# Moving one batch's attention under the weight loads, and spacing attention steps evenly, in a fused attention and feed-forward kernel

## The chip, the cores and the metric

The kernel runs on one core of one Trainium2 chip. The metric is the time of one execution on the device in microseconds (us). Every time below is the median of several executions. A profile is one execution, and its span is about 2 us shorter than the time that the same execution is given as a run. All instants below are us from the start of that span.

Engines are named as in the profile: PE is the matrix engine, DVE the vector engine, ACT the scalar engine, POOL is GpSimd, and SPq is the queue that issues most of the loads.

## The reference

Sliding-window causal attention with a window of 64, then LayerNorm and a two-layer feed-forward with a residual:

```python
# q, k, v: (8, 8, 576, 64) float32;  g_ln: (512,);  w_ch1: (512, 2048);  w_ch2: (2048, 512)
rel    = pos[:, None] - pos[None, :]
mask   = (rel >= 0) & (rel < 64)
scores = np.where(mask, q @ k.T / 8, -1e9)           # per batch and head
x      = softmax(scores) @ v                         # -> (8, 576, 512), heads side by side
xn     = (x - mean(x)) / sqrt(var(x) + 1e-6) * g_ln
out    = x + np.maximum(xn @ w_ch1, 0) @ w_ch2       # (8, 576, 512) float32
```

## The kernel before

The 8 x 576 rows are 36 blocks of 128 rows (`kblk`), in nine groups of four. A batch is 4.5 blocks, so a batch ends in the middle of a block. All matrix products are in float16.

A group's feed-forward is 32 units of four matmuls of 512 columns each: 16 units of layer 1 (`hps`, one per 128 hidden channels) and 16 of layer 2 (`ch`, four per block). The attention of the next batch is put between the units. `at(i, f)` means: issue `f` after unit `i`. In these traces an engine's instructions begin in the order in which they are issued: in the kernel before, for example, a cast on GpSimd whose data had landed at 59.23 us began at 60.84 us, after the cast issued before it (58.76 to 60.65); and PE began layer 2 at 62.38 us, after transposes issued before it, though the last cast of W2 had ended at 54.39 us and the last Relu at 56.48.

```python
    def s_mm(b, ws):            # scores of up to two windows of 64, all heads, then exp on ACT
        ...
    def s_mask(b, ws):          # DVE: pt = pt * mask
        ...
    def b_step(kblk):           # PE: xps = pt @ [v, 1]; then on DVE, one after the other:
        ...                     #   rcp, xn = xps * rcp, bn_stats, bn_aggr, z = (xn - mean) * g
    def zt_step(kblk, eng=None):# PE: transposes z; DVE (or ACT) copies the result to zT
        ...
    for g in range(NGRP):
        units = mlp_units(g)
        ...
        b = g + 1
        at(13, group_stats, g)                      # 1/sqrt(var) of the group, mostly on GpSimd
        if g == 0:
            at(12, t_rem, 0)                        # transposes of batch 0's last 64 rows of q, k
            at(12, cast_qk_rem, 1)
            ...
            t0, s0, sp = 10, 20, 2                  # batch 1 in group 0: steps of 2 units, from 20 on
        else:
            t0, s0, sp = 0, 6, 3                    # steps of 3 units, at 6, 9, 12, 15, 18
        if b < B:
            ...
            for i, ws in enumerate(sets):           # five sets: [0], [1,2], [3,4], [5,6], [7,8]
                at(s0 + sp * i, s_mm, b, ws)
                at(s0 + sp * i + 1, s_mask, b, ws)
            for kblk in range(first, last):
                si = s0 + sp * ((lastw + 1) // 2) + 3
                at(min(si, 32), b_step, kblk)
                at(max(min(si + 4, 32), 17 if kblk // 4 > b else 0), zt_step, kblk)
        if b + 1 < B:                               # loads and GpSimd casts of the batch after that
            ...
            at(22, load_v, n, 0, 4)
            ...
            at(30, cast_v, n, 0, 4)
```

Before group 0, GpSimd is given, in this order: the casts of W1, of batch 1's q and k, of batch 0's remainder, of W2, and of batch 1's V. In the prologue the shifted copy of V (`vB`: the same rows, moved by 64 partitions) is made by DMA from the cast `vA`.

The softmax here doesn't subtract the row's maximum and nothing guards it: scores larger than these inputs give would overflow.

## Time and profile before

The time before is 387.1 us (three runs, 386.42 to 387.87). The timeline of PE gives the first matmul of layer 1 of each group:

| group | 0 | 1 | 2 | 3 | 4 | 5 | 6 | 7 | 8 | end of PE |
|---|---|---|---|---|---|---|---|---|---|---|
| start, us | 37.02 | 92.04 | 132.30 | 171.30 | 209.64 | 248.65 | 286.99 | 324.48 | 352.25 | 380.18 |
| length, us | 55.02 | 40.26 | 39.00 | 38.34 | 39.01 | 38.34 | 37.49 | 27.77 | 27.93 | |

Group 7 has no attention to do. Its 128 matmuls of 512 columns take 27.77 us, or 217 ns each. PE is busy for all of the 27.77 us, at a granted clock of 1.00, and no group is shorter. That is taken here as PE's floor.

The page of the kernel before. First the busy time of each engine and its share of the span. Then the clock that PE was granted, in tenths of full speed, in 40 equal slices. Last, by engine, the chain of waits that ended last:

```profile
PE 323.3 (84%) x2768; PEld 162.6 (42%) x2768; DVE 189.6 (49%) x350; ACT 140.4 (37%) x247; POOL 121.9 (32%) x216
...
PEclk9999996996999999999999999999999999999999
...
PE 55%; DVE 26%; DMA 8%; SPq 6%; issue 3%; POOL 1%; ACT 0%; POOLq 0%
```

DVE is busy for only half of the span, yet it holds a quarter of the chain of waits. So it is the limit in stretches, not on average. The two sixes in the clock are the slices around 60 and 90 us: PE stood still there, and then ran at a lower clock.

The wait view of the kernel before, PE's waits: what waited, its line, what released it, then us in total, times, and the longest. The 5.8 us for the first load are left out:

```profile
PE tpr_697 L192 <- POOL qkr_0_1_616 L104: 5.7, 1, 5.7
PE xps_337 L238 <- DMA vB_188<-vA_133: 3.6, 1, 3.6
...
PE xps_466 L238 <- DVE pt_7_420 L221: 2.3, 1, 2.3
...
PE xps_2037 L238 <- DVE pt_7_1967 L221: 1.4, 1, 1.4
```

They belong to three stages. The second and the third are in the prologue: the V shift by DMA, and a mask. The last is one of the waits for masks (`pt`) that come back in every group from 1 to 6. The first is explained by the timeline of group 0 (start, length, engine, line, operation; in brackets the engine's idle time before it and what ended that):

```profile
58.76 1.89 POOL L125 CAST vA_276<-v_1_261 128x2048 f16<-128x2048 f32 x1 [4.14 <-DMA v_1_261<-in_v_dram]
...
60.84 0.60 POOL L104 CAST qkr_0_1_616<-qk32r_1_270 64x512 f16<-64x512 f32 x1
...
61.50 0.39 PE L192 MATMUL tpr_697<-ident_99,qkr_0_1_616 64*128 64x64 f16 x4 [5.66 <-POOL qkr_0_1_616 L104]
...
62.38 0.61 PE L315 MATMUL ch_0_708<-w2s,hrT_503 128*128 128x512 f16 x1
```

A small cast of batch 1's remainder stood on GpSimd behind the cast of a V that landed late. PE's transposes of that remainder stood in front of layer 2. So layer 2 could not start before 62.38 us.

Windows of the kernel before. The columns are length, busy time (and count) of PE, PEld, DVE, ACT and POOL, PE's granted clock, DMA share, and GB/s:

```profile
61.50:66.00 4.50, 4.33 (x19) 1.86 (x20) 0.49 (x2) 0.00 (x0) 3.75 (x13) 0.59 1.14 323
72.00:92.04 20.04, 12.21 (x179) 6.56 (x180) 19.23 (x36) 3.26 (x6) 6.44 (x10) 0.93 0.59 150
132.30:171.30 39.00, 35.37 (x341) 18.12 (x340) 24.89 (x46) 15.74 (x28) 12.34 (x23) 1.00 0.57 134
```

From 72 to 92 us DVE is busy for 19.23 of 20.04 us with batch 1's attention while PE works for 12. In group 2 PE is idle for 3.6 us of 39, spread over the waits for masks.

Three lines of the timeline of group 2 show part of why DVE is late there. In quiet places of the same trace `z` takes 0.75 us and the mask 0.69 us (for example at 75.25 and 75.92 us). Here both are longer, and GpSimd is casting beside them:

```profile
154.47 1.07 DVE L255 SCALAR_TENSOR_TENSOR z_1939<-xn_1915,mvg_1510,gB 128x512 f16<-128x512 f32 x1
...
154.94 1.50 POOL L95 CAST qk_1_4_0_2094<-qk_1_4_0_1849 128x1024 f16<-128x1024 f32 x1
...
155.46 1.52 DVE L221 TENSOR_TENSOR pt_5_1896<-pt_5_1896,mask 128x1024 f16<-128x1024 f16 x1
```

Of the group's four waits for masks, the two long ones (1.3 and 1.4 us) follow DVE instructions lengthened like this; before the other two (0.4 and 0.6 us) `z` and the mask have their usual lengths.

### The profile page before, as it was taken

The numbers are of one execution on the slowest core, as the hardware profiler recorded it, in microseconds if no ns is written. First come the engines' busy times: TensorE is split into PE (matmuls) and PEld (weight loads), VectorE is DVE, ScalarE is ACT, GpSimd is POOL, SyncE is SP. The second block draws the span as 40 slices with busy tenths as digits, with TensorE's granted clock in tenths as the row PEclk, the third lists the DMA queues.
The fourth block names the chain that finished last, engine by engine and source line by source line (L and its number), as shares of the span: only waits on it lengthen the run. The fifth ranks groups of instructions, "written<-read, shape, count | busy, mean of one in ns | idle before, by whom it ended". The sixth has DMA issues, their size and how long they took to land.

```text
span 384.1 us, 6774 instructions
## 1 busy us (share of the span) xinstructions
PE 323.3 (84%) x2768; PEld 162.6 (42%) x2768; DVE 189.6 (49%) x350; ACT 140.4 (37%) x247; POOL 121.9 (32%) x216
## 2 busy tenths in 40 slices
PE   2444985965997999799979997999799989999995
PEld 1332442433543454345434543454345444444442
DVE  1266030895369438943594379535953794002011
ACT  2421560311671177107710771077107710621610
POOL 4756748640026401630164017311722110101000
PEclk9999996996999999999999999999999999999999
DMA  8999899956301892189318920894073001002002
GB/s 253 274 322 272 304 250 270 202 133 210 71 2 46 170 280 49 34 174 259 80 32 175 294 43 23 183 237 103 24 184 90 2 29 64 19 27 84 0 27 82
DMA packets 73918, 51.62 MB, mean 134 GB/s; under 512 B 47632, under 2 KB 64016, under 8 KB 73888
## 3 DMA queue, kind: packets, MB, share of 16 engines
q1 hardware_dynamic: 72528, 46.41, 46.3%
q0 software_dynamic: 1360, 4.79, 5.8%
q8 instruction: 21, 0.34, 0.4%
q14 instruction: 9, 0.07, 0.1%
HBM read 36.96 MB, written 9.44 MB: 121 GB/s over the span
## 4 chain that ended last, share of the span: by engine, by line
PE 55%; DVE 26%; DMA 8%; SPq 6%; issue 3%; POOL 1%; ACT 0%; POOLq 0%
SPq L114 3%; DMA w1s_125<-in_moe_w_ch_dram 3%; DMA w2s_234<-in_moe_w_ch_dram 2%; DMA qk_0_1_1_214<-in_q_dram 2%; DMA qk32r_1_272<-in_k_dram 1%; PE ch_0_708 L315 1%; SPq L79 1%; PE ch_3_4604 L315 1%; PE ch_2_2087 L315 1%; PE ch_1_4564 L315 1%; PE ch_3_4413 L315 1%; PE ch_1_4373 L315 1%; PE ch_2_4196 L315 1%; PE ch_2_3667 L315 1%; PE ch_3_3185 L315 1%
## 5 line engine op out<-in xcount | busy, mean ns | idle before, releaser
L302 PEld LDWEIGHTS <-w1g 128*128 128x128 f16 x576 | 53.8, 99 | 59.4 <-issue 6.0
L315 PEld LDWEIGHTS <-hrT_4433 128*128 128x128 f16 x64 | 6.3, 98 | 7.6
L315 PEld LDWEIGHTS <-hrT_4242 128*128 128x128 f16 x64 | 6.2, 98 | 7.6
L321 DVE SCALAR_TENSOR_TENSOR osb_4370<-ch_0_4353,rstdg_4327,xn_3495 128x512 f32<-128x512 f32 x1 | 0.8, 751 | 16.2 <-PE ch_0_4353 L315 16.2
L321 DVE SCALAR_TENSOR_TENSOR osb_4561<-ch_0_4544,rstdg_4518,xn_3949 128x512 f32<-128x512 f32 x1 | 0.8, 750 | 16.2 <-PE ch_0_4544 L315 16.2
L315 PEld LDWEIGHTS <-hrT_503 128*128 128x128 f16 x64 | 5.8, 103 | 6.8 <-issue 1.9
L176 DVE COPY qkT_1_571<-tp_1_0_589 128x1024 f16<-128x1024 f16 x1 | 1.2, 1225 | 14.9 <-PE tp_1_0_589 L183 14.9
L290 POOL TENSOR_TENSOR rstmp_1316<-rstdg_1315 128x4 f32<-128x4 f32 x2 | 0.8, 386 | 24.5 <-DVE rstdg_1315 L285 24.4
L290 POOL TENSOR_TENSOR rstmp_4519<-rstdg_4518 128x4 f32<-128x4 f32 x2 | 0.4, 198 | 25.4 <-DVE rstdg_4518 L285 25.3
L315 PEld LDWEIGHTS <-hrT_3729 128*128 128x128 f16 x64 | 5.8, 98 | 6.0
L315 PEld LDWEIGHTS <-hrT_2665 128*128 128x128 f16 x64 | 5.8, 98 | 6.0
L315 PEld LDWEIGHTS <-hrT_1085 128*128 128x128 f16 x64 | 5.8, 98 | 6.0
L315 PEld LDWEIGHTS <-hrT_3213 128*128 128x128 f16 x64 | 5.8, 98 | 6.0
L315 PEld LDWEIGHTS <-hrT_1601 128*128 128x128 f16 x64 | 5.8, 98 | 6.0
L315 PEld LDWEIGHTS <-hrT_2149 128*128 128x128 f16 x64 | 5.8, 97 | 6.0
L306 ACT ACTIVATE hrT_3729<-hps_0_3730 128x512 f16<-128x512 f32 x1 | 0.6, 597 | 15.5 <-PE hps_0_3730 L302 15.5
L306 ACT ACTIVATE hrT_3213<-hps_0_3214 128x512 f16<-128x512 f32 x1 | 0.6, 597 | 15.5 <-PE hps_0_3214 L302 15.5
L306 ACT ACTIVATE hrT_2665<-hps_0_2666 128x512 f16<-128x512 f32 x1 | 0.6, 597 | 15.5 <-PE hps_0_2666 L302 15.5
L306 ACT ACTIVATE hrT_1601<-hps_0_1602 128x512 f16<-128x512 f32 x1 | 0.6, 597 | 15.5 <-PE hps_0_1602 L302 15.5
L306 ACT ACTIVATE hrT_2149<-hps_0_2150 128x512 f16<-128x512 f32 x1 | 0.6, 597 | 15.5 <-PE hps_0_2150 L302 15.5
L290 POOL TENSOR_TENSOR rstmp_2922<-rstdg_2921 128x4 f32<-128x4 f32 x2 | 0.8, 386 | 17.2 <-DVE rstdg_2921 L285 17.2
L290 POOL TENSOR_TENSOR rstmp_1858<-rstdg_1857 128x4 f32<-128x4 f32 x2 | 0.8, 386 | 17.2 <-DVE rstdg_1857 L285 17.1
(1309 smaller groups left out, 931.4 us busy)
## 6 DMA issues: line engine op xcount, KB each, us to landing
v_0_113<-in_v_dram SPq DMA_DIRECT2D x4, 256.0 KB, 7.4
v_1_261<-in_v_dram SPq DMA_DIRECT2D x4, 256.0 KB, 6.9
v_2_784<-in_v_dram SPq DMA_DIRECT2D x4, 256.0 KB, 6.3
v_3_1524<-in_v_dram SPq DMA_DIRECT2D x4, 256.0 KB, 4.4
v_4_2073<-in_v_dram SPq DMA_DIRECT2D x4, 256.0 KB, 4.5
v_5_2589<-in_v_dram SPq DMA_DIRECT2D x4, 256.0 KB, 4.3
v_6_3137<-in_v_dram SPq DMA_DIRECT2D x4, 256.0 KB, 4.3
v_7_3653<-in_v_dram SPq DMA_DIRECT2D x4, 256.0 KB, 5.8
```

Source lines behind the costliest of these rows:

```text
L79: nc.sync.dma_start(out=t[:, :].rearrange("p h j d -> p h (j d)"), in_=src[b, 4 * half:4 * half + 4, 0:512, :].rearrange("h (p j) d -> p h ...
L114: nc.sync.dma_start(out=v32[b][:, c], in_=v[b, :, 128 * c:128 * c + 128, :].rearrange("h s d -> s h d"),)
L176: nc.vector.tensor_copy(out=out, in_=in_)
L290: nc.gpsimd.tensor_tensor(out=ab, in0=rs, in1=rs, op=ALU.mult)
L302: nc.tensor.matmul(out=hps, lhsT=w1g[:, kc, 128 * hc:128 * (hc + 1)], rhs=zT[g][:, kc, :], start=(kc == 0), stop=(kc == NKC - 1),)
L306: nc.scalar.activation(out=hrT[:, hc, :], in_=hps, func=AF.Relu, bias=0.0, scale=1.0)
L315: nc.tensor.matmul(out=ch[kb], lhsT=hrT[:, hc, 128 * kb:128 * (kb + 1)], rhs=w2s[:, hc, :], start=(hc == 0), stop=(hc == NHC - 1),)
L321: nc.vector.scalar_tensor_tensor(out=o, in0=ch[kb], scalar=rstd[g][:, kb:kb + 1], in1=x_norm[kblk][:, :, :].rearrange("p h d -> p (h d)"), ...
```

## The change

The intent has four parts:

1. **Prologue.** The mask becomes a product on PE, a large negative bias written into the scores by an identity matmul, so DVE no longer multiplies masks there. DVE copies replace the DMA that shifts V.
2. **Group 0.** Batch 1's scores run during layer 1 of group 0 and its DVE chain during layer 2. Batch 1 is loaded and cast before W2. Layer 2 of group 0 runs chunk by chunk over the hidden channels in four PSUM banks, so that each chunk of W2 is used as it lands.
3. **Groups 1 to 6.** The attention steps stand five units apart (2, 7, 12, 17, 22) instead of three. Loads and casts of the next batch come earlier, and so do its transposes: they now stand in layer 2 of the group before.
4. **Evacuations.** Copies of transposes out of PSUM move from DVE to ACT.

```diff
+    def make_vB0(c):                       # the V shift, now on DVE
+        nc.vector.tensor_copy(out=vB[0][64:128, c, :, 0:D], in_=v32[0][0:64, c])
+        nc.vector.tensor_copy(out=vB[0][0:64, c + 1, :, 0:D], in_=v32[0][64:128, c])
 ...
+        if pe_mask:                        # in s_mm: the mask as a product
+            for par in range(2):
+                nc.tensor.matmul(out=sc[par]..., lhsT=ident16, rhs=mb, start=True, stop=False, ...)
 ...
+        def l2_hc(i):                      # layer 2 of group 0, two hidden chunks for all four blocks
+            if i == 0:
+                for kb in range(4):
+                    pool, tag = (ps_mm, "mm") if kb < 2 else (ps_s, "sc")
+                    ch[kb] = pool.tile([128, DM], FP32, tag=tag, name=f"ch_{g}_{kb}")
+            for hc in (2 * i, 2 * i + 1):
+                for kb in range(4):
+                    nc.tensor.matmul(out=ch[kb], lhsT=hrT[:, hc, ...], rhs=w2s[:, hc, :], ...)
+            if i == NHC // 2 - 1:
+                for kb in range(4):
+                    add_out(kb)
 ...
+    (prologue: W1, batch 1, its remainder and its V come before)
+    for i in range(8):
+        w2_load(i)
+        w2_cast(i)
 ...
         if g == 0:
+            at(8, t_main, 1, 0, 0, 1)
 ...
             at(12, t_rem, 0)
             at(12, cast_qk_rem, 1)
-            ...
-            t0, s0, sp = 10, 20, 2
+            for i, j in enumerate((12, 13, 14, 15)):
+                at(j, s_mm, 1, SETS[i])
+                at(j, s_mask, 1, SETS[i])
+                ...
+            at(20, t_rem, 1)
+            sb = [17, 18, 19, 20, 21]
+            at(17, group_stats, 0)
         else:
-            t0, s0, sp = 0, 6, 3
+            ss = [2, 7, 12, 17, 22]
+            sb = [x + 3 for x in ss]
+            at(13, group_stats, g)
 ...
-            at(22, load_v, n, 0, 4)
-            at(24, cast_qk, n, 0)
-            at(30, cast_v, n, 0, 4)
+            e = 16 if g > 0 else 12
+            at(e - 6, load_v, n, 0, 4)
+            at(e - 1, cast_qk, n, 0)
+            at(e + 5, cast_v, n, 0, 4)
+            at(e + 8, t_main, n, 0, 0, 0)   # the last argument: evacuate on ACT
 ...
```

More of the change, by code (lines that the diff above doesn't have):

```diff
@@ L64 @@
     mask = p_const.tile([128, 64], FP16, tag="mask", name="mask")
+    mbias = p_const.tile([128, 64], FP16, tag="mbias", name="mbias")
     magt = p_const.tile([128, 4], FP32, tag="magt", name="magt")
@@ L176, in evac, with t_main @@
             nc.vector.tensor_copy(out=out, in_=in_)
-    def t_main(b, x, half):
+    def t_main(b, x, half, eng=None):
         src = qk16.pop((b, x, half))
@@ L183, in t_main, with t_rem @@
                 nc.tensor.transpose(out=tp[:, i, j, :], in_=src[:, i, j], identity=ident16)
-        evac(x, qkT[b][x][:, 2 * half:2 * half + 2, 64 * x:64 * x + 512].rearrange("c i (p j) -> c i p j", j=4),
+        evac(x if eng is None else eng, qkT[b][x][:, 2 * half:2 * half + 2, 64 * x:64 * x + 512].rearrange("c i (p j) -> c i p j", j=4),
              tp[:, :].rearrange("c i j p -> c i p j"))
-    def t_rem(b):
+    def t_rem(b, eng=1):
         tp = ps_t.tile([128, 2, NHP, 64], FP16, tag="tp", name=f"tpr_{b}")
@@ L194, in t_rem, with s_mm @@
         for x in range(2):
-            nc.vector.tensor_copy(out=qkT[b][x][:, :, 64 * x + 512:64 * x + S], in_=tp[:, x])
-    def s_mm(b, ws):
+            evac(eng, qkT[b][x][:, :, 64 * x + 512:64 * x + S], tp[:, x])
+    def s_mm(b, ws, pe_mask=False):
         nw = len(ws)
@@ L200, in s_mm @@
         pt = p_pt.tile([128, 2, NHP, nw, 64], FP16, tag=f"pt{nw}", name=f"pt_{b}_{ws[0]}", bufs=6 if nw == 2 else 3)
+        if pe_mask:
+            m = mbias[:, :]
+            mb = bass.AP(tensor=m.tensor, offset=m.offset, ap=[m.ap[0], [0, NHP * nw], m.ap[1]])
+            for par in range(2):
+                nc.tensor.matmul(
+                    out=sc[par][:, :].rearrange("p h w i -> p (h w) i"), lhsT=ident16, rhs=mb,
+                    start=True, stop=False, skip_group_check=True,
+                )
         for hp in range(NHP):
@@ L208, in s_mm @@
                         rhs=qkT[b][0][rows, hp, 64 * w:64 * w + 64],
-                        start=True, stop=True,
+                        start=not pe_mask, stop=True, skip_group_check=pe_mask,
                     )
@@ L293, in group_stats, with mlp_units @@
             nc.gpsimd.tensor_tensor(out=rs, in0=rs, in1=ab, op=ALU.mult)
-    def mlp_units(g):
+    def mlp_units(g, hc_outer=False):
         hrT = p_hrt.tile([128, NHC, 512], FP16, tag="hrT", name=f"hrT_{g}")
@@ L319, in l2, with add_out @@
             if part == 3:
+                add_out(kb)
+        def add_out(kb):
+                kblk = 4 * g + kb
                 o = p_blk.tile([128, DM], FP32, tag="osb", name=f"osb_{kblk}")
@@ L328, in mlp_units @@
             units.append(lambda hc=hc: l1(hc))
+        def l2_hc(i):
[5 more added lines that the diff above has]
+                for kb in range(4):
+                    nc.tensor.matmul(
+                        out=ch[kb], lhsT=hrT[:, hc, 128 * kb:128 * (kb + 1)], rhs=w2s[:, hc, :],
+                        start=(hc == 0), stop=(hc == NHC - 1),
+                    )
+            if i == NHC // 2 - 1:
+                for kb in range(4):
+                    add_out(kb)
+        if hc_outer:
+            for i in range(NHC // 2):
+                units.append(lambda i=i: l2_hc(i))
+            return units
         for kb in range(4):
@@ L352 @@
     )
+    nc.vector.tensor_scalar(out=mbias, in0=mask, scalar1=-1.0, scalar2=30000.0, op0=ALU.add, op1=ALU.mult)
     alloc_qkT(0)
@@ L360 @@
     alloc_vB(0)
+    nc.gpsimd.memset(vB[0][:, :, :, D:D + 1], 1.0)
+    nc.gpsimd.memset(vB[0][0:64, 0, :, D:D + 1], 0.0)
     for c in range(4):
         cast_v(0, c, c + 1)
-        if c % 2 == 1:
-            make_vB(0, c - 1, c + 1)
+    sets0 = [[0], [1, 2], [3, 4], [5, 6], [7]]
+    s_mm(0, sets0[0], True)
+    make_vB0(0)
+    s_mm(0, sets0[1], True)
+    make_vB0(1)
+    for i in range(2, 5):
+        s_mm(0, sets0[i], True)
+        b_step(i - 2)
+        if i < 4:
+            make_vB0(i)
+        if i >= 3:
+            zt_step(i - 3, "act")
+    b_step(3)
+    zt_step(2, "act")
+    zt_step(3, "act")
     for i in range(4):
@@ L373 @@
         w1_cast(i + 4)
-        w2_load(i)
     cast_qk(1, 0)
@@ L378 @@
     cast_v_rem(0)
-    for i in range(4):
-        w2_cast(i)
-        w2_load(i + 4)
     load_v(1, 0, 4)
-    for i in range(4):
-        w2_cast(i + 4)
     load_qk_rem(1)
@@ L387 @@
     alloc_v(1)
+    alloc_vB(1)
+    alloc_qkT(1)
+    make_vB(0, 4, 5)
     cast_v(1, 0, 4)
-    sets0 = [[0], [1, 2], [3, 4], [5, 6], [7]]
-    s_mm(0, sets0[0])
-    s_mm(0, sets0[1])
-    s_mask(0, sets0[0])
-    for i in range(2, 5):
-        s_mm(0, sets0[i])
-        s_mask(0, sets0[i - 1])
-        b_step(i - 2)
-        if i >= 3:
-            zt_step(i - 3, "act")
-    s_mask(0, sets0[4])
-    b_step(3)
-    zt_step(2, "act")
-    zt_step(3, "act")
+    cast_v_rem(1)
+    make_vB(1, 0, 5)
@@ L405 @@
+    for i in range(8):
+        w2_load(i)
+        w2_cast(i)
+    SETS = [[0], [1, 2], [3, 4], [5, 6], [7, 8]]
     for g in range(NGRP):
-        units = mlp_units(g)
+        units = mlp_units(g, g == 0)
         slots = [[] for _ in range(len(units) + 1)]
         def at(i, f, *a):
-            slots[i].append((f, a))
+            slots[min(i, len(slots) - 1)].append((f, a))
         b = g + 1
-        at(13, group_stats, g)
         if g == 0:
+            at(8, t_main, 1, 0, 0, 1)
+            at(9, t_main, 1, 1, 0, 1)
+            at(10, t_main, 1, 0, 1, 1)
+            at(11, t_main, 1, 1, 1, 1)
@@ L415 @@
             at(12, t_rem, 0)
             at(12, cast_qk_rem, 1)
-            at(12, cast_v_rem, 1)
-            at(14, make_vB, 0, 4, 5)
-            at(14, s_mm, 0, [8])
-            at(15, s_mask, 0, [8])
-            t0, s0, sp = 10, 20, 2
-        else:
-            t0, s0, sp = 0, 6, 3
-        if b < B:
-            at(t0, alloc_qkT, b)
-            at(t0 + 0, t_main, b, 0, 0)
-            at(t0 + 1, t_main, b, 1, 0)
-            at(t0 + 2, t_main, b, 0, 1)
-            at(t0 + 3, t_main, b, 1, 1)
-            at(t0 + 5, t_rem, b)
-            at(s0 - 1, alloc_vB, b)
-            at(s0 - 1, make_vB, b, 0, 5)
-            sets = [[0], [1, 2], [3, 4], [5, 6], [7, 8]]
-            for i, ws in enumerate(sets):
-                at(s0 + sp * i, s_mm, b, ws)
-                at(s0 + sp * i + 1, s_mask, b, ws)
-            first, last = (NW * b) // 2, (NW * (b + 1)) // 2
-            for kblk in range(first, last):
-                lastw = (2 * kblk + 1) - NW * b
-                si = s0 + sp * ((lastw + 1) // 2) + 3
-                at(min(si, 32), b_step, kblk)
-                at(max(min(si + 4, 32), 17 if kblk // 4 > b else 0), zt_step, kblk)
+            for i, j in enumerate((12, 13, 14, 15)):
+                at(j, s_mm, 1, SETS[i])
+                at(j, s_mask, 1, SETS[i])
+                if i == 0:
+                    at(14, s_mm, 0, [8])
+                    at(14, s_mask, 0, [8])
@@ new lines @@
+            at(20, t_rem, 1)
+            sb = [17, 18, 19, 20, 21]
+            at(17, group_stats, 0)
+        else:
+            ss = [2, 7, 12, 17, 22]
+            sb = [x + 3 for x in ss]
+            at(13, group_stats, g)
+        if g == 1:
+            at(0, s_mm, 1, SETS[4])
+            at(0, s_mask, 1, SETS[4])
+            at(3, b_step, 8)
+            at(7, zt_step, 8, "act")
+        if b < B:
+            if g > 0:
+                for i, ws in enumerate(SETS):
+                    at(ss[i], s_mm, b, ws)
+                    at(ss[i] + 1, s_mask, b, ws)
+                at(0, alloc_vB, b)
+                at(0, make_vB, b, 0, 5)
+            for kblk in range((NW * b) // 2, (NW * (b + 1)) // 2):
+                if kblk == 8 and g == 0:
+                    continue
+                si = sb[((2 * kblk + 1) - NW * b + 1) // 2]
+                at(si, b_step, kblk)
+                dz = 2 if g == 0 else 4
+                at(max(si + dz, 17 if kblk // 4 > b else 0), zt_step, kblk, "act")
@@ L443 @@
         if b + 1 < B:
             n = b + 1
-            at(12, load_qk, n, 0)
-            at(14, load_qk, n, 1)
-            at(16, load_qk_rem, n)
-            at(22, load_v, n, 0, 4)
-            at(22, load_v_rem, n)
-            at(24, cast_qk, n, 0)
-            at(26, cast_qk, n, 1)
-            at(28, cast_qk_rem, n)
-            at(30, alloc_v, n)
-            at(30, cast_v, n, 0, 4)
-            at(30, cast_v_rem, n)
+            e = 16 if g > 0 else 12
+            at(e - 12, load_qk, n, 0)
@@ new lines @@
+            at(e - 11, load_qk, n, 1)
+            at(e - 10, load_qk_rem, n)
+            at(e - 6, load_v, n, 0, 4)
+            at(e - 6, load_v_rem, n)
+            at(e - 1, cast_qk, n, 0)
+            at(e + 1, cast_qk, n, 1)
+            at(e + 3, cast_qk_rem, n)
+            at(e + 5, alloc_v, n)
+            at(e + 5, cast_v, n, 0, 4)
+            at(e + 6, cast_v_rem, n)
+            at(e + 5, alloc_qkT, n)
+            at(e + 8, t_main, n, 0, 0, 0)
+            at(e + 10, t_main, n, 1, 0, 0)
@@ L456 @@
+            at(e + 12, t_main, n, 0, 1, 0)
+            at(e + 13, t_main, n, 1, 1, 0)
+            at(e + 15, t_rem, n, 0)
         for i, u in enumerate(units):
```

## The prediction

> **What bounds the kernel now.** The timeline gives the first matmul of each group's layer 1: group 0 at 37.0 us, group 1 at 92.0, then 132.3, 171.3, 209.6, 248.6, 287.0, 324.5, 352.2; the span ends at 384.1. Three regimes:
>
> - Groups 7 and 8 have no attention and take 27.7 us: 128 matmuls of 512 columns at 216 ns.[...] This is PE's floor.
> - Groups 1 to 6 take 37.5 to 40.3 us, 38.75 on average. Without PE's waits they would need about 35.2: the wait view shows in groups 2 to 4 some 3 to 3.7 us each of `xps` matmuls waiting for DVE's masks (1.4, 1.3, 0.7, 0.4 us). A step has three units of 0.86 us; DVE needs 3.4 us for it.
> - Before 92 us (windows): DMA is saturated (about 270 GB/s). Group 0's layer 2 can't start until 62.4: the `tpr` transposes ahead of it wait 5.7 us for a GpSimd cast behind a late V load. From 72 to 92 the chain of waits is batch 1's attention on DVE with PE half idle.
>
> **What the change does.**
> 1. Prologue: the V shift goes from DMA to DVE copies (the first `xps` waited 3.6 us for it). Masks leave DVE's chain (three waits of 2.1 to 2.3 us); two wide identity matmuls per score set[...] are added on PE, which has room. DVE's chain keeps 2.55 us a block plus about 1.1 us of copies (estimate, from the 0.6 us casts of the same size). Layer 1 of group 0 should start near 33 instead of 37.
> 2. Batch 1's scores run in layer 1 of group 0, its DVE chain in layer 2, behind the W2 loads. The bytes up to W2's end are nearly the same: W2 lands at 58 to 60 us, consumed chunk by chunk. PE's order holds a trap: `t_rem(1)` stands before the last three chunks, and its cast stands on GpSimd behind all W2 casts and the cast of batch 2's first half. That comes at 65 us, the end of layer 2 at about 71, `group_stats` (behind two more casts) at about 73, and group 1 at 73.5 instead of 92: 18.5 us gained.
> 3. Group 1 gets `kblk` 8 and batch 2's late V: 37.5 us, 3 us gained.
> 4. Groups 2 to 6: five units per step instead of three, and evacuations moved to ACT (layer 1: about 14 us of ACT work in 16). The mask waits go; 35.1 us each, against 38.4: about 17 us gained.
> 5. Groups 7 and 8 and the tail: the same 59.8 us.
>
> 73.5 + 37.5 + 5 x 35.1 + 59.8 = 346.3 us of span; a run takes about 3 us more than the span of the profile: 349.5 us.
>
> Nearly all is critical: group starts are PE's own order.
>
> **What would show it.** First `hps` of group 0 at 33, of group 1 at 71 to 77, steps of 35 us up to group 7; PE busy about 93%; `xps` waits on `pt` gone.
>
> **What would make it wrong.** W2 landing later[...]; the GpSimd order in group 0 costing more; ACT late with the Relu in layer 1; batch 2's V stalling group 1.
>
> Predicted 349.5 us, 8 in 10 between 342 and 359. Faster by over 2%: 0.96; within: 0.03; slower: 0.01.

Three passages are cut from it, as no trace or run here shows them: a figure for a matmul that was not taken from the trace, the length of the mask's two matmuls, and a reason why W2 might land later. None is a term of its sum, which stands whole: 73.5 + 37.5 + 5 x 35.1 + 59.8 = 346.3 us of span. In the trace after, the mask's matmuls of the first full score set take 0.95 us of PE (14.23 to 15.18 us). Saturated is a DMA share of 1.02 at 271 GB/s from 0 to 72 us in the trace before; from 72 to 92 us the share is 0.59.

## The result

The kernel after takes 353.86 us (four runs, 351.5 to 354.45), and in the same rounds the kernel before takes 387.49 us (four runs, 386.42 to 387.98). The ratio is 0.9124, with a 95% interval from 0.9077 to 0.9171. Ratios in this document are the mean time of one kernel's runs over that of the other's of the same rounds, so they are not quite the ratio of the medians quoted. Executions over 1.5% slower than the fastest of the same kernel are left out of the means.

| | group 0 starts | group 1 starts | group 1 | groups 2 to 6, mean | group 7 | group 7's start to the span's end | span |
|---|---|---|---|---|---|---|---|
| before | 37.02 | 92.04 | 40.26 | 38.44 | 27.77 | 59.6 | 384.1 |
| predicted | 33 | 73.5 | 37.5 | 35.1 | | 59.8 | 346.3 |
| after | 35.55 | 80.26 | 36.54 | 35.05 | 27.77 | 59.6 | 351.7 |

Of the 32.4 us of span, 1.5 us went before group 0, 10.3 us in group 0, 3.7 us in group 1, and 16.9 us in groups 2 to 6. Nothing changed after group 7's start. Two parts of this sum are not what they seem. In the kernel before, group 1 began with 3.91 us at a clock of 0.50, so about 2 us of its gain is a lower clock that is gone (an estimate, half of 3.91: four matmuls of 512 columns take 1.71 us there, 92.04 to 93.75 us, and 0.86 us in group 7). And each batch's transposes now stand one group earlier: group 6 has none left (PE is busy in it for 33.47 us, x303, instead of 35.36, x341), and group 0 has those of batch 2 in addition. So about 2 us of what groups 2 to 6 gained are work moved into group 0.

The page after, the same three lines:

```profile
PE 323.0 (92%) x2778; PEld 159.5 (45%) x2778; DVE 169.0 (48%) x300; ACT 172.9 (49%) x301; POOL 120.5 (34%) x214
...
PEclk9999999999999999999999999999999999999998
...
PE 82%; DVE 7%; DMA 4%; SPq 3%; ACT 3%; issue 0%; POOL 0%
```

PE's busy time is the same to 0.3 us, so what went is idle time of PE. The two slices with a low clock are gone. DVE's part of the chain fell from 26% to 7%.

Windows after, layer 2 of group 0 up to group 1's start, and then group 2:

```profile
56.84:80.26 23.42, 20.00 (x197) 10.72 (x193) 18.65 (x31) 6.83 (x11) 17.09 (x27) 1.00 0.79 231
116.80:152.53 35.73, 35.72 (x343) 17.86 (x341) 20.15 (x38) 21.32 (x37) 12.66 (x22) 1.00 0.59 147
```

In group 2 PE is now busy for 35.72 of 35.73 us, and no `xps` waits for a mask any more. What PE still waits for, in the wait view after, is almost all before group 1. These are the longest after the first load's 5.8 us:

```profile
PE ztp_429 L280 <- DVE z_421 L268: 2.5, 1, 2.5
PE tp_0_0_997 L188 <- DVE qkT_1_494 L181: 1.9, 1, 1.9
PE xps_398 L251 <- DVE xn_365 L260: 1.8, 1, 1.8
```

The first and the third are in the prologue, the second in group 0's layer 2. The timeline of that stretch:

```profile
63.14 1.04 POOL L171 CAST w2s<-w2s_523 128x1024 f16<-128x1024 f32 x1 [0.34 <-DMA w2s_523<-in_moe_w_ch_dram]
64.94 1.04 POOL L96 CAST qk_0_2_0_658<-qk_0_2_0_533 128x1024 f16<-128x1024 f32 x1 [0.75 <-DMA qk_0_2_0_533<-in_q_dram]
66.12 1.04 POOL L96 CAST qk_1_2_0_660<-qk_1_2_0_535 128x1024 f16<-128x1024 f32 x1
...
67.11 1.07 POOL L105 CAST qkr_0_1_679<-qk32r_1_483 64x512 f16<-64x512 f32 x1
...
68.23 0.29 PE L197 MATMUL tpr_954<-ident_99,qkr_0_1_679 64*128 64x64 f16 x4 [0.33 <-POOL qkr_0_1_679 L105]
...
69.53 1.72 DVE L268 SCALAR_TENSOR_TENSOR z_944<-xn_920,mvg_860,gB 128x512 f16<-128x512 f32 x1
...
71.17 0.28 DVE L181 COPY qkT_1_493<-tpr_954 128x256 f16<-128x256 f16 x1
...
71.70 0.62 PE L188 MATMUL tp_0_0_997<-ident_99,qk_0_2_0_658 128*128 128x128 f16 x8 [1.92 <-DVE qkT_1_494 L181]
```

The pattern of before is there again, only smaller. The remainder's cast (line 105) stands on GpSimd behind all of W2's casts and behind casts of batch 2, and these wait for data that land late: the last of W2 at 63.1 us, batch 2's first q and k at 64.5 and 66.0 us. PE's transposes come at 68.23 us. DVE then evacuates them only after a `z` that took 1.72 us instead of 0.75. PE waits 1.92 us for the buffer.

The other place is the prologue, in the timeline after:

```profile
20.62 1.59 DVE L268 SCALAR_TENSOR_TENSOR z_288<-xn_263,mvg_286,gB 128x512 f16<-128x512 f32 x1
20.63 1.04 POOL L159 CAST w1g<-w1s_124 128x1024 f16<-128x1024 f32 x1 [0.31 <-DMA w1s_124<-in_moe_w_ch_dram]
...
21.93 1.18 POOL L159 CAST w1g<-w1s_126 128x1024 f16<-128x1024 f32 x1 [0.26 <-DMA w1s_126<-in_moe_w_ch_dram]
22.24 1.15 DVE L136 CAST vB_190<-v_0_114 64x512 f16<-64x512 f32 x1
```

`z` and the new V copy are long just where GpSimd casts W1: 1.59 us for `z` beside a cast of 1.04, and 1.15 us for the copy beside one of 1.18. The second copy, which begins at 23.41 us between two casts, takes 0.42 us. Whether the casts are the cause, and what it costs, is left to the experiments.

### The profile page after: what moved, and what is told of

Same layout as the page of the kernel before. It is cut to its first block, busy times and chain, and to the rows that moved or that the text cites. A ratio compares the mean times of both kernels' runs of the same rounds, so it can differ in the third digit from the quotient of the medians.

```text
span 351.7 us, 6792 instructions
## 1 busy us (share of the span) xinstructions
PE 323.0 (92%) x2778; PEld 159.5 (45%) x2778; DVE 169.0 (48%) x300; ACT 172.9 (49%) x301; POOL 120.5 (34%) x214
## 4 chain that ended last, share of the span: by engine, by line
PE 82%; DVE 7%; DMA 4%; SPq 3%; ACT 3%; issue 0%; POOL 0%
DMA w1s_124<-in_moe_w_ch_dram 2%; SPq L115 2%; DMA w1s_442<-in_moe_w_ch_dram 1%; PE ch_1_4109 L328 1%; PE ch_1_3592 L328 1%; PE ch_1_2526 L328 1%; PE ch_1_3076 L328 1%; PE ch_1_2010 L328 1%; PE ch_0_1954 L328 1%; PE ch_0_1406 L328 1%; PE ch_0_3535 L328 1%; PE ch_0_3019 L328 1%; PE ch_0_2470 L328 1%; PE ch_1_1462 L328 1%; PE ch_2_3667 L328 1%; PE ch_2_4177 L328 1%
## 5 line engine op out<-in xcount | busy, mean ns | idle before, releaser
L328 PEld LDWEIGHTS <-hrT_4446 128*128 128x128 f16 x64 | 6.3, 98 | 7.5
L328 PEld LDWEIGHTS <-hrT_4255 128*128 128x128 f16 x64 | 6.2, 98 | 7.6
L353 PEld LDWEIGHTS <-hrT_526 128*128 128x128 f16 x64 | 5.8, 98 | 6.7 <-issue 0.8
L328 PEld LDWEIGHTS <-hrT_3796 128*128 128x128 f16 x64 | 5.8, 98 | 5.8
L328 PEld LDWEIGHTS <-hrT_2216 128*128 128x128 f16 x64 | 5.7, 98 | 5.4
L328 PEld LDWEIGHTS <-hrT_1668 128*128 128x128 f16 x64 | 5.6, 98 | 5.4
L328 PEld LDWEIGHTS <-hrT_2732 128*128 128x128 f16 x64 | 5.6, 98 | 5.4
L328 PEld LDWEIGHTS <-hrT_3280 128*128 128x128 f16 x64 | 5.6, 98 | 5.4
L328 PEld LDWEIGHTS <-hrT_1096 128*128 128x128 f16 x64 | 5.6, 98 | 5.4
L319 ACT ACTIVATE hrT_4446<-hps_0_4447 128x512 f16<-128x512 f32 x1 | 0.6, 597 | 14.1 <-PE hps_0_4447 L315 14.1
L188 PE MATMUL tp_0_0_146<-ident_99,qk_0_0_0_142 128*128 128x128 f16 x8 | 1.0, 311 | 5.8 <-POOL qk_0_0_0_142 L96 5.8
```

Source lines behind the costliest of these rows:

```text
L188: nc.tensor.transpose(out=tp[:, i, j, :], in_=src[:, i, j], identity=ident16)
L319: nc.scalar.activation(out=hrT[:, hc, :], in_=hps, func=AF.Relu, bias=0.0, scale=1.0)
L328: nc.tensor.matmul(out=ch[kb], lhsT=hrT[:, hc, 128 * kb:128 * (kb + 1)], rhs=w2s[:, hc, :], start=(hc == 0), stop=(hc == NHC - 1),)
L353: nc.tensor.matmul(out=ch[kb], lhsT=hrT[:, hc, 128 * kb:128 * (kb + 1)], rhs=w2s[:, hc, :], start=(hc == 0), stop=(hc == NHC - 1),)
```

## The experiments

The theory had three parts. Spacing is what gains in groups 2 to 6, not the evacuations. Group 0's gain is the moved attention, held back by the order of GpSimd's queue. The prologue's shortfall is DVE's copies held up beside GpSimd. The rivals were: ACT's taking over of evacuations gains in the groups; the four banks, with W2 used as it lands, gain in group 0; and the prologue sets the start of group 1. Each kernel below gives the right result. Starts and lengths of groups are from the timelines of PE.

| label | median, us | runs | ratio to before | group 0 starts | group 1 starts | group 2, us |
|---|---|---|---|---|---|---|
| the change | 353.86 | 4 | 0.9124 [0.9077, 0.9171] | 35.55 | 80.26 | 35.73 |
| u_spacing | 389.23 | 4 | 1.0017 [0.9922, 1.0112] | 35.37 | 78.71 | 42.39 |
| u_evac | 351.93 | 4 | 0.9069 [0.9007, 0.9132] | 33.71 | 77.38 | 35.74 |
| u_hc | 360.36 | 4 | 0.9294 [0.9227, 0.9361] | 36.04 | 86.71 | 35.73 |
| g0_old | 365.93 | 4 | 0.9439 [0.9363, 0.9514] | 36.22 | 95.57 | 35.73 |
| u_mask | 355.64 | 6 | 0.9187 [0.9146, 0.9229] | 38.45 | 81.45 | 35.73 |
| u_vdma | 355.40 | 6 | 0.9166 [0.9122, 0.9209] | 33.39 | 81.84 | 35.73 |
| vb_act | 353.97 | 6 | 0.9142 [0.9105, 0.9179] | 32.08 | 80.14 | 35.73 |
| w1_act | 353.90 | 6 | 0.9146 [0.9111, 0.9180] | 32.29 | 79.55 | 35.73 |
| after_again | 351.82 | 6 | 0.9072 [0.9034, 0.9111] | 34.56 | 78.11 | 35.73 |
| trem | 350.99 | 6 | 0.9046 [0.9007, 0.9086] | 33.69 | 75.75 | 35.73 |
| best | 351.14 | 6 | 0.9055 [0.9014, 0.9095] | 30.52 | 76.58 | 35.73 |
| sp3_vlate | 371.25 | 6 | 0.9556 [0.9510, 0.9602] | 35.71 | 80.21 | 39.05 |

The four from u_spacing to g0_old ran in one job (before: 387.11 us), the four from u_mask to w1_act in a second (386.86), the last four in a third (388.57). The same kernel gave 353.86 us and 351.82 us in two jobs, and ratios of 0.9124 and 0.9072. So differences of 2 us between jobs mean nothing. Four of the expected times below were missed by less than that (u_evac, u_mask, u_vdma, the control). Nor is a group's start fixed: u_evac has the same instructions as the change up to group 1, and together with the two profiles of the change itself it shows group 1 starting at 80.26, 78.11 and 77.38 us.

### u_spacing: the steps three units apart again

```diff
-            ss = [2, 7, 12, 17, 22]
+            ss = [6, 9, 12, 15, 18]
```

> The changed kernel with the attention steps of groups 1 to 7 three units apart again (6, 9, 12, 15, 18), evacuations still late and on ACT. Theory (the even spacing removed the mask waits): the xps matmuls wait for DVE's masks again, about 3 us a group, groups 2 to 6 take about 38 us instead of 35.05, the run about 370 us (+16). Rival (moving the evacuations off DVE and out of layer 1 did it): groups stay at 35 to 35.7 us, the run at 354 to 357.

It took 389.23 us, so the whole gain was gone: the direction was right, but the loss of some 35 us was more than twice the 16 expected. Groups 1 to 5 take 42.3 to 43.3 us, longer than in the kernel before (38.3 to 40.3), though the spacing is the same. The wait view of u_spacing names the wait, the timeline names what is beside it, and the windows show what came after:

```profile
PE xps L251 <- DVE pt L234: 28.2, 20, 3.4
```

```profile
146.97 3.00 DVE L268 SCALAR_TENSOR_TENSOR z<-xn,mvg,gB 128x512 f16<-128x512 f32 x1
...
147.53 1.91 POOL L126 CAST vA<-v 128x2048 f16<-128x2048 f32 x1
...
151.29 0.26 PE L251 MATMUL xps<-vA,pt 128*64 128x65 f16 x1 [3.36 <-DVE pt L234]
```

```profile
147.00:151.20 4.20, 0.94 (x5) 0.20 (x3) 4.20 (x3) 0.00 (x0) 4.20 (x7) 0.97 0.00 0
151.20:156.00 4.80, 4.71 (x34) 2.44 (x35) 3.31 (x7) 0.58 (x1) 0.95 (x3) 0.67 0.66 179
```

The changed kernel casts V at unit 21. With steps at 6 to 18 a `z` falls on that cast and takes 3.00 us instead of 0.75. It began at 146.97 us, before the cast of V (147.53 to 149.44), and ended at 149.97, after it; that is one event. The mask behind it is late, and PE waits 3.36 us. The granted clock is then 0.67 over the next 4.8 us, so more than the wait was lost. A lower clock did not follow every long gap of PE in these traces. It followed this one of 3.36 us, and in w1_act (a run below) one of 2.55 us (the clock is the third number from the end):

```profile
68.02 0.29 PE L197 MATMUL tpr<-ident,qkr 64*128 64x64 f16 x4 [2.55 <-POOL qkr L105]
```

```profile
65.07:68.48 3.41, 0.70 (x6) 0.17 (x4) 2.32 (x4) 0.00 (x0) 2.95 (x5) 1.00 0.66 210
68.48:71.90 3.42, 3.23 (x35) 2.36 (x36) 2.14 (x6) 1.25 (x2) 2.63 (x4) 0.50 0.64 142
```

In best, also below, it was 0.50 after a gap of 1.41 us. But it stayed at 1.00 after a gap of 2.37 us in the kernel before (80.45 to 82.83 us), and in group 2 there with its waits of at most 1.4 us. So the length of a single gap does not decide it in these traces; what does was not tested.

So u_spacing undid one thing and brought in another. That called for a run that undoes the spacing without the collision.

### sp3_vlate: three units apart, with V loaded and cast as late as before

```diff
-            ss = [2, 7, 12, 17, 22]
+            ss = [6, 9, 12, 15, 18]
-            at(e - 6, load_v, n, 0, 4)       # unit 10 in groups 1 and later
+            at(22 if g > 0 else e - 6, load_v, n, 0, 4)
-            at(e + 5, cast_v, n, 0, 4)       # unit 21
+            at(30 if g > 0 else e + 5, cast_v, n, 0, 4)
         (and the same for the rest of V)
```

> Three-unit steps as in the run that took 389 us, but with the next batch's V loaded from unit 22 and cast after it, as in the kernel before. Theory (with three units DVE has no slack, and the early 1.9 us V cast on GpSimd stopped z for 3.0 us, with PE waiting 3.4 us and its clock dropping): groups 2 to 6 go from 42.8 to 38.5 to 39.5 us, the run to 362 to 367. Rival (the evacuations moved to ACT do not suit three-unit steps): groups stay at 42 to 43, the run at 385 or more.

It took 371.25 us, against 351.82 us for the change in the same job. Groups 2 to 5 take 39.05, 38.38, 39.04 and 38.38 us: the lengths of the kernel before (39.00, 38.34, 39.01, 38.34) to 0.05 us. The groups are close to what was expected; the total is 4 us above the 362 to 367 written, a range that did not fit its own group lengths (five groups of 38.5 us and more instead of 35.05 are over 17 us on top of some 352). Its wait view:

```profile
PE xps L251 <- DVE pt L234: 18.5, 20, 1.4
```

So the even spacing, with the early V for which it makes room, is worth 19.0 us of the medians of the fast runs. By the profiles, groups 1 to 6 together take 232.4 us before, 229.9 in sp3_vlate and 211.8 in the control: the spacing has 18.1 of the 20.6 us, as much as the waits for masks in sp3_vlate (18.5 us). Most of the other 2.5 us is in group 6 (37.49 before, 35.31 in sp3_vlate), whose transposes sp3_vlate too has moved to group 5. Two things were not run: five units with the late V, and three units with the casts of q and k moved away from DVE's `z` and masks. So how much of the 18.1 us is room as such and how much is room to absorb lengthened instructions stays open. That it absorbs them is shown: in group 2 of the change `z` still takes up to 1.43 us and the mask up to 1.05, and PE does not wait. The spacing does a second thing. It makes room for the early cast of V, which at three units costs about 18 us more (u_spacing against sp3_vlate, in different jobs).

### u_evac: the evacuations of groups 1 and later on DVE again

```diff
-                at(..., zt_step, kblk, "act")
+                at(..., zt_step, kblk, "act" if g == 0 else None)
-            at(e + 10, t_main, n, 1, 0, 0)
+            at(e + 10, t_main, n, 1, 0, 1 if g > 0 else 0)
         (and the same for the second half and for t_rem)
```

> The changed kernel with the evacuations of groups 1 to 7 back on DVE (transposed z, transposed k, the remainder), the spacing of five units kept. Theory (spacing): DVE has slack in five units, groups 2 to 6 stay within 0.4 us of 35.05, the run at 353 to 356. Rival (ACT offload): waits on masks come back, groups at 37 to 38, the run at 364 to 370.

The steady groups are the same: 35.74, 35.16, 35.73, 35.16 and 33.48 us. The rival falls. At five units DVE has room enough, and moving copies to ACT gains nothing. At three units it seems to gain nothing either: sp3_vlate evacuates on ACT and has, in groups 2 to 5, the lengths of the kernel before, which evacuates mostly on DVE.

### g0_old: batch 1's attention in group 0's layer 2, as before

```diff
-        units = mlp_units(g, g == 0)
+        units = mlp_units(g)                  # blocks one after the other, two banks
-            for i, j in enumerate((12, 13, 14, 15)):
-                at(j, s_mm, 1, SETS[i])
-                at(j, s_mask, 1, SETS[i])
-            at(20, t_rem, 1)
-            sb = [17, 18, 19, 20, 21]
+            at(15, t_rem, 1)
+            for i in range(5):
+                at(20 + 2 * i, s_mm, 1, SETS[i])
+                at(21 + 2 * i, s_mask, 1, SETS[i])
+            sb = [23, 25, 27, 29, 31]
         (and group 1's extra block back in group 0; batch 2's loads and transposes four units later)
```

> The changed kernel with batch 1's attention put back into group 0's layer 2 as before (transposes at units 10 to 13, remainder at 15, scores from unit 20, block 8 in group 0, block order of layer 2). Theory (attending batch 1 under the W2 load is the larger part of the early gain): group 1 starts at 90 to 96 us instead of 80.3, the run at 364 to 370. Rival (the prologue and the earlier V load give most of the early gain): group 1 at 81 to 84, the run at 355 to 358.

It took 365.93 us, and group 1 starts at 95.57 us. Layer 2 starts at 65.75 us, right after the same transposes as in the kernel before:

```profile
64.87 0.39 PE L197 MATMUL tpr<-ident,qkr 64*128 64x64 f16 x4 [10.19 <-POOL qkr L105]
```

The remaining parts of the change, with the old group 0, leave group 1 later than before (92.04). So the new load order alone, with W2 behind batch 1, makes the old group 0 longer (59.3 us instead of 55.0, of which batch 2's transposes are about 2), and group 0 gains only together with its reordering. What the moved attention and the four banks have in it apart from each other this run does not tell, as it undid both.

### u_hc: group 0's layer 2 block by block in two banks

```diff
-        units = mlp_units(g, g == 0)
+        units = mlp_units(g)
-            slots[min(i, len(slots) - 1)].append((f, a))
+            if g == 0 and i > 16:
+                i = 16 + 2 * (i - 16)          # the same places in 32 units
+            slots[min(i, len(slots) - 1)].append((f, a))
-            at(17, group_stats, 0)
+            at(13, group_stats, 0)
```

The last line was not wanted. With `group_stats` at 17 the block order would deadlock by the reading of the kernel, because it needs the result in the middle of layer 2.

> The changed kernel with group 0's layer 2 block by block in two banks as before (all else in its place; group_stats issued four units earlier, as the block order would deadlock otherwise). Theory (W2 must be consumed as it lands): the last W2 cast ended at 64.2 us and layer 2 began at 56.8, so the first block waits about 4 us; group 1 starts at 84, the run at 358. Rival (in the changed kernel PE is busy or held by other things in layer 2, W2 is never awaited, so the order is worth little): 354 plus or minus 1.5.

It took 360.36 us, and group 1 starts at 86.71 us. The theory had put it at 84 us, from a wait for W2 alone. The waits for W2 are small (1.8 us in three waits). The larger cost is elsewhere, in its timeline:

```profile
70.62 0.75 DVE L338 SCALAR_TENSOR_TENSOR osb<-ch,rstdg,xn 128x512 f32<-128x512 f32 x1 [5.54 <-POOL rstdg L306]
...
72.27 0.26 PE L251 MATMUL xps<-vA,pt 128*64 128x65 f16 x1 [4.47 <-DVE xn L260]
```

In block order the first block's output is due a quarter of the way through layer 2. It needs `rstd`, which GpSimd computes behind the casts of W2, of batch 2's first half and of the remainder. DVE stood still for 5.54 us, and PE, which waits for DVE, then for 4.47. In this order of GpSimd's queue the four banks gain less by reaching W2 early than by putting all outputs at the end, when `rstd` is there. Block order with `group_stats` in front of W2's casts was not run.

### u_mask and u_vdma: the two parts of the prologue undone, one at a time

```diff
# u_mask
-    s_mm(0, sets0[0], True)
+    s_mm(0, sets0[0])
+    s_mask(0, sets0[0])                       # DVE multiplies the mask; the same for the other sets
# u_vdma
-    make_vB0(i)                               # all four DVE copies
+        if c % 2 == 1:
+            make_vB(0, c - 1, c + 1)          # the DMA shift, as before
```

> The changed kernel with the prologue's masks back on DVE (a product after the exp) instead of identity matmuls into the score banks. Theory (DVE's chain sets the start of group 0): four masks, 0.42 to 0.69 us alone and up to twice that beside a GpSimd cast, come back into the chain; layer 1 of group 0 starts 2 to 4 us later, the run at 356 to 358. Rival (PE's wide mask matmuls, about 1.2 us a set[...], cost as much): 353 to 355.

> The changed kernel with the V shift of batch 0 by DMA again, no DVE copies. Theory (DVE's chain, not the DMA, is what matters): the first xps comes at about 20 us instead of 18, but each block loses 0.84 to 1.57 us of copies, so layer 1 starts no later than 35.5, the run at 352 to 354. Rival (the DMA wait of 3.6 us was on the path, as the change assumes): start at 37, the run at 356 to 358.

The mask on DVE moves group 0's start to 38.45 us, the latest of all. The V shift by DMA does not: 33.39 us, so in these profiles DVE's copies bring no earlier start than the DMA. Yet group 1 starts at 81.45 and 81.84 us, close to the change's 80.26, and the times are 355.64 and 355.40 us. The second job had no control of its own, so no difference to the change of below about 2 us is claimed from it.

### vb_act and w1_act: is DVE held up by GpSimd's casts, and does it matter?

vb_act gives the V copies to ACT. w1_act leaves them on DVE but moves the casts of W1 from GpSimd to ACT, which takes the suspected cause away.

```diff
# vb_act
-        nc.vector.tensor_copy(out=vB[0][64:128, c, :, 0:D], in_=v32[0][0:64, c])
+        nc.scalar.copy(out=vB[0][64:128, c, :, 0:D], in_=v32[0][0:64, c])
         (and the other copy)
# w1_act
-        nc.gpsimd.tensor_copy(out=w1g[...], in_=t)
+        nc.scalar.copy(out=w1g[...], in_=t)
         (issued two at a time between the steps of the prologue)
```

> The changed kernel with the four shifted copies of V on ACT instead of DVE. Theory (DVE's chain): two pairs of copies of 1.57 us leave the chain between the blocks, layer 1 of group 0 starts near 32.5 instead of 35.5 and the run takes 350 to 351.5. Rival (W1's arrival or PE bounds the start): no change, 353 to 354.

> The changed kernel with the eight W1 casts of the prologue on ACT instead of GpSimd, put between the attention steps. Theory[...]: with GpSimd silent, z takes 0.75 us instead of 1.3 to 1.6, the longer V copy 0.42 instead of 1.15; layer 1 starts near 32, the run at 350 to 351.5. Rival (DVE is slowed by the DMA traffic or by the crossing of partitions): z stays at 1.3 and the copies at 1.15, no gain.

The timeline of w1_act, at the place shown of the change:

```profile
20.64 0.75 DVE L268 SCALAR_TENSOR_TENSOR z<-xn,mvg,gB 128x512 f16<-128x512 f32 x1
21.42 0.42 DVE L136 CAST vB<-v 64x512 f16<-64x512 f32 x1
```

With GpSimd idle `z` is 0.75 us instead of 1.59, and the copy 0.42 instead of 1.15. So GpSimd's casts are what stretched them. The stretch is inside the recorded length of a DVE instruction and counts as busy: around the `z` of 3.00 us in u_spacing DVE is busy for 4.20 of 4.20 us. On ACT the copy takes 0.62 us each time. Group 0 starts at 32.29 and 32.08 us, 1.4 to 3.5 us earlier than in the three profiles of the change's own prologue (35.55, 34.56 and u_evac's 33.71), and close to the predicted 33.

Still, the times are 353.90 and 353.97 us, not the 350 to 351.5 expected, and group 1 starts at 79.55 and 80.14 us. The wait view of vb_act shows where the lead went:

```profile
PE tpr L197 <- POOL qkr L105: 4.5, 2, 4.3
```

PE came earlier to the remainder's transposes and waited 4.3 us there, where the change waits 0.3 us in each of two waits. After that wait the clock was 0.50 for 3.4 us (from 69.43 us; in w1_act from 68.48). The remainder's cast could not come earlier, because the last cast of W2, in front of it, began at 63.50 and 62.83 us here, no earlier than in the three profiles of the change's own order (63.14, 60.56, 62.28). W2 did not land sooner although group 0 had started sooner. The prologue's shortfall had a real cause, and it was not on the path that sets group 1's start.

### trem and best: the remainder taken out of its place behind W2

trem issues the remainder's cast before W2's casts, puts W2's loads and casts into unit 5, and evacuates the remainder on ACT. best adds vb_act's copies.

```diff
-    for i in range(8):
-        w2_load(i)
-        w2_cast(i)
 ...
-            at(12, t_rem, 0)
-            at(12, cast_qk_rem, 1)
+            at(5, t_rem, 0)
+            at(5, cast_qk_rem, 1)
+            for i in range(8):
+                at(5, w2_load, i)
+                at(5, w2_cast, i)
-            at(20, t_rem, 1)
+            at(20, t_rem, 1, 0)               # evacuated on ACT
         (batch 2's loads of q and k follow at unit 6)
```

> The changed kernel, unedited, as the control for the three others on the same chip. Every theory: 353 to 354.5 us, group 1 from 79 to 81 us.

> The changed kernel with batch 1's remainder taken out of the queue: its q and k casts go before the W2 casts on GpSimd (the transposes of batch 0's remainder move to unit 5 to free the buffer) and its evacuation goes to ACT. Theory (the start of group 1 is set by PE's wait at the remainder's transposes for a cast queued behind W2 and batch 2, and by the DVE evacuation behind z): the waits of 0.6 and 1.9 us go, group 1 starts near 77.5, the run at 351 to 352. Rival (something else, W2 or batch 2's q and k, ends as late): group 1 at 79.5 to 80.5, the run at 353.5.

> The same together with the shifted V copies on ACT, which alone started layer 1 of group 0 at 32.1 us but group 1 no earlier. Theory: with the wait at the remainder gone, the 3 us now pass through; group 1 starts near 75, the run at 348 to 349.5. Rival (a second limit, batch 2's q and k landing at 65 to 67, or W2): group 1 at 77 or later, the run no better than with the first edit alone.

The transposes of batch 1's remainder wait for nothing in trem. In the control's profile they did not wait for GpSimd either, as the last cast of W2 began at 60.56 us there; it has only the wait for DVE's copy, of 1.38 us. Group 1 starts at 75.75 us, against 78.11 us in the control's profile, then takes 37.42 instead of 36.54 us. The times, 350.99 and 351.14 us, cannot be told from the control's 351.82 us. A new wait stands where the old one was. First the timeline of trem, then that of best:

```profile
74.84 2.73 DVE L338 SCALAR_TENSOR_TENSOR osb<-ch,rstdg,xn 128x512 f32<-128x512 f32 x4 [3.59 <-POOL rstdg L306]
```

```profile
75.78 1.41 DVE L338 SCALAR_TENSOR_TENSOR osb<-ch,rstdg,xn 128x512 f32<-128x512 f32 x2 [5.27 <-POOL rstdg L306]
...
76.58 0.38 PE L315 MATMUL hps<-zT,w1g 128*128 128x512 f16 x1 [1.41 <-DVE osb L338]
```

Group 0's outputs now wait for `rstd`, whose small operations stand on GpSimd behind batch 2's casts, and in best group 1's first matmul waits for those outputs. The clock was 0.50 from 76.96 to 80.37 us after that, and group 1 took 38.34 us. So best, expected at 348 to 349.5 us with group 1 near 75, came out nearer to its rival, a second limit. So neither version beats the change by an amount that these runs can show. Moving `group_stats` of group 0 in front of W2's casts is the next step by these lines. It was not run, so what it would bring stays open.

## Why the prediction was right, and where its sizes were off

The time, 353.86 us, is inside the range of 342 to 359 us and 4.4 us above the centre of 349.5 us.

- **Step 4, groups 2 to 6: right.** Predicted 35.1 us each, measured 35.05 on average; that it fits so closely is partly luck, as groups 2 to 5 take 35.45 us and group 6, which lost its transposes, 33.48. "The mask waits go": the wait view has none left. The prediction named spacing and evacuations together. The runs give nothing of it to the evacuations (u_evac has the same groups) and nearly all to the spacing: groups 2 to 6 take 192.2 us before, 190.2 in sp3_vlate and 175.3 after.
- **Step 3, group 1: right in the main.** 37.5 us predicted, 36.54 measured. The lower clock at its start before, worth about 2 us, was not in the argument.
- **Step 5: right.** 59.8 us predicted, 59.6 measured.
- **Step 1, the prologue: a term mis-sized.** "About 1.1 us of copies" measured 1.15 + 0.42 = 1.57 us at the place shown, and `z` took 1.27 to 1.59 us instead of 0.75 in three of the four blocks. They stand beside GpSimd's casts; at the place shown w1_act, with W1's casts on ACT, has 0.75 and 0.42 us. Group 0 started at 35.55 us instead of 33, and at 34.56 in the second profile. But vb_act and w1_act show that group 1 gains nothing from a mended prologue, so this miss cost next to nothing.
- **Step 2, group 0: the mechanism right, terms mis-sized.** The prediction saw the trap, the remainder's transposes behind GpSimd's queue, and put them at 65 us; they came at 68.2 us. Two things were late by nearly the same. PE reached them only at 67.9 us, as layer 1 had started 2.5 us late. And the queue was late because its loads were: W2, put at 58 to 60 us, landed at 63.1, and batch 2's k, in front of the remainder, at 66.0. So to mend one alone gains little: vb_act brought PE there earlier and it waited 4.3 us for the queue; in the control the queue was earlier and PE still came at 67.05 us. From there to group 1 it allowed 8.5 us, and 12.0 us were measured (68.23 to 80.26). Not named in its sum are the wait of 1.92 us for DVE's evacuation of these transposes and the transposes of batch 2 that stand before group 1. It also held `group_stats` to come last. In this kernel its result was there at 76.9 us, before PE was done. It is last only once the remainder is out of the way (trem, best). Group 1 started at 80.26 us (77.4 to 80.3 in three profiles of the same code) instead of 73.5.
- **What would make it wrong.** Of the four fears two came true, and they are one: "W2 landing later" and "the GpSimd order in group 0 costing more". PE never waited for W2 itself, but GpSimd's queue did (63.1 us instead of 58 to 60), and the remainder's cast behind it. Why W2 landed later was not tested. And group 1, which batch 2's V might have stalled, came out shorter than predicted. Of ACT's Relu in layer 1 the wait view shows one wait of 0.2 us.

The sum confirms it: group 1's start was 6.8 us later than predicted, group 1 was 1.0 us shorter, groups 2 to 6 together 0.2 us shorter, and the rest 0.2 us shorter. That makes 5.4 us, which is the span of 351.7 us less the predicted 346.3. A run exceeded its span by 2 us and not by 3, which leaves the 4.4 us.

## What to carry to other kernels

Give each step of the engine that works in order more time than the engine behind it needs before moving work between engines: five units instead of three, with the early V, were worth 18 to 19 us here, and handing copies to ACT nothing. Small pieces (a remainder, a statistic) waited here for everything that was queued before them on their engine (PE stood for 5.7 us at the remainder's cast before, for 10.2 us in g0_old), so list each queue in order and ask who waits for the last small thing; expect that freeing one uncovers the next. And when one part is undone for a test, look for what the rest of the change had placed in its slack, as u_spacing did with the cast of V.
